# One explicit step order grouped by array tiling, and small matmuls padded to the whole array, in a fused attention and token-mixing kernel

## The chip, the cores and the metric

The kernel runs on one core of a Trainium2 chip. The metric is the device time of that core in microseconds (us), the median of several executions, lower is better. Ratios between kernels are computed as the mean time of one kernel's fast runs over the mean time of the other's fast runs in the same rounds on the same chip, so they are not quite the ratios of the medians quoted beside them. The square brackets after a ratio are its 95% interval. A single-core run is called slow when it lies over 1.5% above the fastest run of the same kernel.

The engines are called as the profile calls them: PE multiplies matrices, PEld loads its weights, DVE and ACT are the vector and scalar engines, POOL is the third elementwise engine, SP issues the DMAs (transfers between the chip's large memory and the engines' own). PSUM is the memory that PE writes its results to; copying a result out of it by ACT or DVE is called an eviction.

## The reference, cut to what matters

```python
# q, k, v: (8 batches, 8 heads, 576 positions, 64)
def _attn_ref(q, k, v):
    q_d, k_d, v_d = (means over 4 neighbouring positions)        # 144 positions
    out_d  = softmax(q_d k_d^T / 8) v_d                           # coarse attention
    out_up = np.repeat(out_d, 4, axis=2)
    out_local = softmax(q k^T / 8 where |i - j| < 4) v            # a narrow band
    return out_up + out_local

def _moe_ref(x, w_q, w_k, w_out):                                 # x: (8, 576, 512)
    wq, wk = x @ w_q, x @ w_k                                     # 512 -> 64
    mixed = (wq @ wk^T / 8) @ x
    return np.maximum(mixed, 0.0) @ w_out
```

The kernel works in half precision. It uses that `(wq wk^T) x = wq (wk^T x)`, so it forms the 64x512 matrix `M2 = wk^T x` first.

## The kernel before

For each batch there are three stages, and three batches are in work at a time: stage A of batch i runs together with stage B of batch i-1 and stage C of batch i-2. One such round is called a period here.

| stage | steps (name of the PSUM tile in the profile) |
|---|---|
| casts | POOL turns q, k and v from fp32 to fp16 |
| A | `tq`, `tk`, `tr`: transposes (pq, pk, pr); `sums`: coarse q and k by POOL; `score`: masks, then banded scores (psc); `vd`: coarse v (pv) |
| B | `cs`: coarse scores (pcs); `av`, `ca`: the two attention outputs (pav, pca); `odt`, `xt`: transposes (pod, px) |
| C | `wt` (pw), `wkt` (pwk), `wks` (pwd), `m2` (pm), `mx` and `mxr` (pmx, pmr), `og` and `ol` (po, pol) |

The PE can run as one array of 128x128 or as several smaller tiles. Which form a matmul uses follows from its shape: `wt` runs in 128x128, banded scores in 64x64, coarse scores in 64x128. The profile prints this form behind the operands of every matmul.

Four parts of the program carry the argument. First, only the PE is held to program order; the instructions of ACT, DVE and POOL are ordered by the build's own scheduler:

```python
class _InOrder:
    def __getattr__(self, name):
        f_ = getattr(self._engine, name)
        return lambda *a, **k: self._tc.keep_in_program_order(f_(*a, **k))
...
TEN_ = _InOrder(tc, nc.tensor)
```

Second, the PSUM buffers: every large step takes one of only three two-bank buffers, and the buffer comes free when ACT or DVE has copied it out.

```python
ps2 = ctx.enter_context(tc.tile_pool(name="ps2", bufs=3, space=bass.MemoryType.PSUM))   # ps(): two banks
ps1 = ctx.enter_context(tc.tile_pool(name="ps1", bufs=2, space=bass.MemoryType.PSUM))   # psm(): one bank
```

Third, the order of the steps. Each step has a weight, and `merge` interleaves the three stages so that each advances evenly through the period:

```python
return [(2., wt), (.5, wkt), (.4, wks), (1.5, m2), (.5, mx(0)), (.5, mx(1)), (.3, mxr),
        (1.8, og(0)), (1.8, og(1)), (.9, ol)]
...
for i in range(B + 2):
    ... m_ = [stage_c(i - 2), stage_b(i - 1), stage_a(i), stage_cast(i + 1)]     # shortened
    merge(m_)
```

Fourth, the two POOL steps and the matmul:

```python
def vv():      # stage_cast: cast of v
    nc.gpsimd.tensor_copy(v16[:, :, :, 0:64], v32)
def sums():    # stage A: coarse q and k; reads qT and kT, which tq, tk and tr produce
    nc.gpsimd.tensor_tensor(s_, t4[:, :, :, 0:2], t4[:, :, :, 2:4], op=ALU.add)
    ...
def vd():      # stage A: coarse v on the PE; reads the cast v
    pv = ps(name="pv")
    ...
```

The softmax here doesn't subtract the row's maximum and nothing guards it: scores larger than these inputs give would overflow.

## Time and profile before

The median of three runs was 227.92 us (227.62 to 228.11). In the middle of the run all periods are alike.

| reading, kernel before | value | view |
|---|---|---|
| span of the profiled run | 225.2 us | head of the page |
| period (start of `pw` to the next start of `pw`) | 23.06 us | chain of waits |
| PE, POOL, ACT, DVE busy in a period | 21.5, 13.6, 12.7, 12.1 us | table of windows |
| changes of array tiling in a period | 40 | PE's timeline, counted |
| gap before the first `pv` matmul, start to start | 0.79 us | PE's timeline |

The first lines are from the page of the kernel before: the busy time of each engine, with its share of the span and its instruction count, and the clock that PE was granted in 40 equal slices of the span (9 is 90% or more of full speed).

```profile
PE 180.7 (80%) x2752; PEld 112.2 (50%) x2752; DVE 104.3 (46%) x262; ACT 103.1 (46%) x137; POOL 115.9 (51%) x131
...
PEclk9999999857999999999999999999999999999999
```

The PE is by far the busiest engine, and its clock is full but for two slices early in the run. The next lines are the table of windows of the kernel before, for one period: the stretch and its length, busy time and count of each engine, then granted clock, DMA share and rate.

```profile
core 0: us, PE busy (x) PEld busy (x) DVE busy (x) ACT busy (x) POOL busy (x), PEclk, DMA share, GB/s
121.79:144.85 23.06, 21.51 (x344) 13.35 (x345) 12.07 (x28) 12.68 (x18) 13.57 (x13) 1.00 0.82 213
```

The PE is busy for 21.5 of 23.06 us at full clock. The chain of waits of the kernel before follows, for the same period: start in us, length, engine and what it worked on.

```profile
121.79 2.13 PE pw L27 x16
...
124.30 1.00 PE pq_2292 L27 x16
125.30 0.47 PE pca L27 x10
...
128.09 1.87 ACT kT L184
...
134.39 1.90 PE po L27 x8
136.29 0.99 PE pod L27 x8
137.28 0.69 PE psc L27 x36
138.21 1.83 PE po L27 x8
...
144.85 2.13 PE pw L27 x16
```

In this period PE holds 13.4 of the chain's 23.06 us, ACT and DVE hold 7.3. The long `po` steps of stage C stand between short steps of the other stages, and while the PE works at them the other engines have time to copy. Last, PE's timeline of the kernel before around `pv`: start, length, engine, operation, result<-operands, array tiling, shape, and in brackets the wait and what ended it.

```profile
117.37 0.23 PE L27 MATMUL px<-id_67,x_1811 128*128 128x128 f16 x1
117.44 0.22 PE L27 MATMUL px<-id_67,x_1898 128*128 128x128 f16 x1
...
117.88 0.22 PE L27 MATMUL px<-id_67,x_2135 128*128 128x128 f16 x1
118.67 0.38 PE L27 MATMUL pv<-v_1_138,P_149 128*32 128x512 f16 x1 [0.57 <-POOL v_1_138 L163]
```

Equal neighbours start about 56 ns apart (117.44 to 117.88 holds eight such steps), although each is shown as 220 ns long: matmuls overlap, so the distance from start to start is the cost. The last line: `pv` waits 0.57 us for POOL's cast of v, and so it does, by 0.5 to 0.6 us, in the other full periods.

### The profile page before, as it was taken

How to read it: one execution, taken by the hardware profiler on the slowest of the kernel's cores; microseconds unless marked ns; L12 is line 12 of the kernel's file. 1: busy time of each engine (PE TensorE's matmuls, PEld its weight loads, DVE VectorE, ACT ScalarE, POOL GpSimd, SP SyncE). 2: the span in 40 equal slices, each digit the busy share in tenths (PEclk: the TensorE clock that was granted, in tenths of full speed). 3: DMA queues.
4: the chain of work that ended last, by engine and by line, in shares of the span. 5: the costliest groups of instructions: out<-in, count | busy, mean ns of one | idle time of the engine just before them, and what ended most of it. 6: DMA issues, size and time to landing. Idle time of an engine off the chain costs nothing.

```text
span 225.2 us, 6421 instructions
## 1 busy us (share of the span) xinstructions
PE 180.7 (80%) x2752; PEld 112.2 (50%) x2752; DVE 104.3 (46%) x262; ACT 103.1 (46%) x137; POOL 115.9 (51%) x131
## 2 busy tenths in 40 slices
PE   0336077759988998899898989898989998999681
PEld 0223046536555664566455745574557455656330
DVE  6005046523466337354726472646364546477022
ACT  2154036413843593458444853475456554331331
POOL 3587991993079607970698059904990393000000
PEclk9999999857999999999999999999999999999999
DMA  6999989979974599659974997599731022104105
GB/s 184 288 198 328 317 165 263 266 150 243 249 173 146 156 349 163 194 146 341 170 207 129 332 175 167 189 309 206 195 136 27 3 92 82 41 3 157 53 0 210
DMA packets 74027, 40.54 MB, mean 180 GB/s; under 512 B 52432, under 2 KB 68880, under 8 KB 74000
## 3 DMA queue, kind: packets, MB, share of 16 engines
q1 hardware_dynamic: 73920, 40.12, 68.7%
q8 instruction: 21, 0.34, 0.7%
q14 instruction: 6, 0.05, 0.1%
q10 hardware_dynamic: 80, 0.03, 0.1%
HBM read 30.67 MB, written 9.44 MB: 178 GB/s over the span
## 4 chain that ended last, share of the span: by engine, by line
PE 49%; DVE 17%; POOL 16%; ACT 10%; issue 3%; DMA 3%; POOLq 0%; DVEq 0%; ACTq 0%
PE po L27 11%; PE pw L27 8%; ACT kT L184 5%; DVE xT L368 5%; DVE rmx L445 4%; PE pav L27 3%; PE pmx L27 3%; PE pod L27 3%; DMA q_72<-in_q_dram 3%; PE psc L27 3%; DVE os L470 3%; PE px L27 2%; PE pca L27 2%; POOL qd L207 2%; PE pwd L27 1%
## 5 line engine op out<-in xcount | busy, mean ns | idle before, releaser
L27 PE MATMUL po<-wo_98,rmx 128*128 128x512 f16 x128 | 30.4, 380 | 2.3 <-ACT rmx L443 0.6
L27 PEld LDWEIGHTS <-rmx 128*128 128x128 f16 (+1 forms) x160 | 14.1, 100 | 18.1 <-ACT rmx L443 0.7
L368 DVE COPY xT<-px 128x928 f16<-128x928 f16 (+1 forms) x32 | 14.3, 453 | 11.4 <-PE px L27 11.0
L348 DVE RECIPROCAL rz<-pav 128x8 f32<-128x8 f32 x40 | 8.1, 202 | 24.7 <-PE pav L27 23.9
L27 PEld LDWEIGHTS <-wqk_97 128*128 128x128 f16 x128 | 12.2, 100 | 6.5 <-DVE xT L368 2.9
L313 DVE RECIPROCAL rc<-pca 128x8 f32<-128x8 f32 (+1 forms) x16 | 3.2, 201 | 22.6 <-PE pca L27 22.6
L468 ACT COPY os<-po 128x1024 f32<-128x1024 f32 x8 | 8.1, 1012 | 11.8 <-PE po L27 10.6
L445 DVE TENSOR_SCALAR rmx<-pmx 128x1024 f16<-128x1024 f32 x8 | 9.8, 1224 | 7.3 <-PE pmx L27 7.3
L27 PE MATMUL pw<-odT,wqk_97 128*128 128x288 f16 x64 | 11.0, 297 | 1.5 <-DVE xT L368 1.5
L470 DVE COPY os<-po 128x1024 f32<-128x1024 f32 x8 | 9.7, 1216 | 4.8 <-ACT os L468 3.0
L443 ACT ACTIVATE rmx<-pmx 128x1024 f16<-128x1024 f32 x8 | 8.2, 1024 | 5.9 <-PE pmx L27 5.9
L27 PE MATMUL pw<-xT,wqk_97 128*128 128x288 f16 x64 | 10.8, 293 | 0.0
L27 PE MATMUL psc<-id_67,neg 64*128 64x232 f16 (+1 forms) x80 | 8.7, 280 | 2.1 <-DVE rmx L445 2.1
L329 DVE COPY odT<-pod 128x576 f16<-128x576 f16 x8 | 3.7, 458 | 14.4 <-PE pod L27 14.4
L27 PE MATMUL psc<-qT,kT 64*64 64x58 f16 (+1 forms) x640 | 10.3, 200 | 0.0
L482 ACT COPY ol<-pol 64x512 f32<-64x512 f32 x8 | 4.6, 579 | 11.6 <-PE pol L27 11.6
L27 PEld LDWEIGHTS <-kT 64*64 64x64 f16 x640 | 7.6, 114 | 4.4 <-issue 3.8
L27 PE MATMUL pq_230<-id_67,q_142 128*128 128x128 f16 x16 | 1.9, 312 | 8.6 <-POOL q_142 L156 8.6
L27 PE MATMUL pv<-v_0_136,P_149 128*32 128x512 f16 x3 | 1.3, 449 | 9.0 <-POOL v_0_136 L163 9.0
L27 PE MATMUL pol<-wo_98,rmx 128*64 128x512 f16 x32 | 8.4, 385 | 0.0
L242 ACT ACTIVATE E_0_122<-psc 128x928 f16<-128x928 f32 x4 | 3.8, 946 | 9.7 <-PE psc L27 9.7
L256 ACT CAST vd_0_195<-pv 128x512 f16<-128x512 f32 x4 | 2.4, 588 | 12.5 <-PE pv L27 12.5
(561 smaller groups left out, 518.3 us busy)
## 6 DMA issues: line engine op xcount, KB each, us to landing
out_dram<-os SPq DMA_DIRECT2D x16, 512.0 KB, 3.0
v_75<-in_v_dram SPq DMA_DIRECT2D x10, 128.0 KB, 4.2
v_215<-in_v_dram SPq DMA_DIRECT2D x10, 128.0 KB, 4.4
v_401<-in_v_dram SPq DMA_DIRECT2D x10, 128.0 KB, 3.7
v_779<-in_v_dram SPq DMA_DIRECT2D x10, 128.0 KB, 3.9
v_1258<-in_v_dram SPq DMA_DIRECT2D x10, 128.0 KB, 4.2
v_1737<-in_v_dram SPq DMA_DIRECT2D x10, 128.0 KB, 3.7
v_2216<-in_v_dram SPq DMA_DIRECT2D x10, 128.0 KB, 3.8
```

Of the source, the lines that this page charges most:

```text
L27: return lambda *a, **k: self._tc.keep_in_program_order(f_(*a, **k))
L184: nc.scalar.copy(t_[:, :, 0:512].rearrange("p j (t f) -> p j t f", f=4), g["p" + key].rearrange("p a (j f t) -> p (a j) t f", j=2, f=4))
L207: nc.gpsimd.tensor_tensor(qd, s_[:, :, :, 0], s_[:, :, :, 1], op=ALU.add)
L242: nc.scalar.activation(E.rearrange("p a n h w -> p a (n h) w")[:, :, :, 0:w], p_[:, :, 0:len(pr_) * W].rearrange("p a (x w) -> p a x w", w=w),
L329: nc.vector.tensor_copy(odT, p_[:, 0:4 * T].rearrange("p (r t) -> p r t", r=4))
L348: nc.vector.reciprocal(rz[:, n], _ap(p_, 64, [[row(p_), 128], [512, 2], [65, 4]]))
L368: nc.vector.tensor_copy(g["xT"][:, 2 * i:2 * i + 2, o:o + m * w].rearrange("p r (m w) -> p r m w", m=m), p_[:, :, lo:lo + 64 * m].rearrang ...
L443: nc.scalar.activation(d_, p_, ACTF.Relu)
L445: nc.vector.tensor_scalar_max(d_, p_, 0.0)
L468: nc.scalar.copy(os_, p_)
L470: nc.vector.tensor_copy(os_, p_)
L482: nc.scalar.copy(ol_, p_[0:64])
```

## The change

The intent: changing the form of the array costs PE time, and there are 40 changes in a period. The change writes all steps of all stages in one list, in which steps of equal tiling stand together, and it pads small matmuls so that they run in the form of their neighbours. The diff, cut to its core:

```diff
+    ORDER = [                                     # (offset of the batch, step)
+        (3, "load_qk"), (2, "load_v"), (0, "sums"),
+        (-2, "wt"),
+        (0, "mask0"), (-1, "cs0"), (0, "score0"), (-1, "av0"), (-1, "av3"),
+        (1, "tq"),
+        (0, "mask1"), (-1, "cs1"), (-2, "wks"), (-2, "wkt"), (0, "score1"), (-1, "av1"), (-1, "av2"),
+        (1, "tk"), (-1, "ca0"), (1, "tr"), (-2, "m2"),
+        (2, "cast_qk"),
+        (0, "mask2"), (0, "score2"), (-1, "av4"),
+        (-1, "ca1"), (-2, "mx0"), (-2, "mx1"), (-2, "mxr"), (-1, "xt0"), (-1, "odt"),
+        (1, "cast_v"),
+        (0, "vd"), (-1, "xt1"),
+        (-2, "og0"), (-2, "og1"), (-2, "ol"),
+    ]
...
-    for i in range(B + 2):
...
-        merge(m_)
+    for i in range(-1, B + 2):
+        for lag, name in ORDER:
+            b = i + lag
+            if 0 <= b < B and (b, name) not in done:
+                steps[b][name]()
```

The padding, one example of each kind (the coarse scores' tail, the summed keys, `mx`, `ol`):

```diff
-                        TEN_.matmul(p_[32 * hl:32 * hl + 32, p, 2 * T:3 * T],
-                                         kd[64 * p:64 * p + 64, hl, 128:160], ...          # 64x32
+                        pe.matmul(p_[:, p, 2 * T:3 * T],
+                                  kdt[64 * p:64 * p + 64, 128 * hl:128 * hl + 128], ...     # 64x128
-            for i, M in ((0, 128), (1, T - 128)):                                          # wks
-                    TEN_.matmul(p_[0:M, 64 * i:64 * i + 64],
+            for i in range(2):
+                    pe.matmul(p_[:, 64 * i:64 * i + 64],
-                    TEN_.matmul(p_[:, rr, :], M2[:, 128 * r:128 * r + 128], wT[0:64, 0:512], # mx
+                    pe.matmul(p_[:, rr, :], M2[:, 128 * r:128 * r + 128], wT[:, 0:512],
-                TEN_.matmul(p_[0:64], rmx[:, r, 512:S], wo16[:, r, :],                      # ol
+                pe.matmul(p_, rmx[:, r * S + 512:r * S + 640], wo16[:, r, :],
```

In the same way the second `ca` step and the `odt` transposes go from 16 rows to 128, and `m2` from 64 columns to 128. Loads of q and k are issued three batches ahead and of v two; before, all were one ahead.

## The prediction

> **What bounds the kernel now.** After the start, a batch takes 23.06 us: in the chain of waits `pw` starts at 98.73, 121.79, 144.85 us. The table of windows gives, for each such period, PE 21.5 us busy, POOL 13.6, ACT 12.7, DVE 12.1. PE in order is the bound. In PE's timeline, start to start, equal neighbours follow at about N/2.4 ns (512 columns 216 ns, 128 columns 56), but the last matmul before a change of array tiling holds PE some 95 ns longer (a transpose 151 instead of 56). The Trainium skill ("TensorEngine Tiling (Array Packing)", Key Properties) says that changing the tiling mode drains the engine; the trace agrees, with 95 ns. I count 40 changes a period: 3.8 us. Waits cost about 1.7 us more (`pv` on the cast of v 0.6, `psc` on `rmx` 0.3).
>
> **What the change removes and adds.** Explicit order and padding leave 11 changes a period: 29 fewer, -2.8 us. Padding costs little, since a matmul is paid by its moving columns: `odT` transposes +0.2 us (but eight changes gone), coarse scores +0.1. PE's own work would fall to about 19 us a period.
>
> **Why I do not expect that gain.** Only PE is held to program order. The built program shows how the other engines are ordered:
> - PSUM: three two-bank buffers. Before, long `po` and `pm` steps lie between short ones. Now the short ones that need ACT or DVE copies stand together: `wt`, cs0, score0, av0, av3, tq, cs1, score1, av1, av2, tk. ACT must do 0.64+0.89+0.95+1.87+0.64+0.26+0.8+0.95+1.87 = 8.9 us there, against about 6 us of PE work.
> - DVE: the copy `os` of the second output half (1.2 us) mostly stands in the next period, behind the `av` and `ca` evictions. It keeps one of the three buffers for some 20 us, so two rotate.
> - POOL: `sums` of batch i+1 (about 7.1 us, after `tr`) stands before the cast of v of batch i (2.3 us), for which `vd` of the same period waits.
>
> So a cycle closes: `vd` to `ol` 5 us, `wt` to `tr` about 13 us with the buffer waits (8.5 without), `rem` copy 0.6, `sums` 7.1, cast 2.3: up to 28.
>
> Estimate: both built orders with their waits, set end to end with durations from this trace. Kernel before: 22.6 a period (measured 23.06), so I add 2%. Kernel after: 25.8 to 28.6. The first `wt` comes at about 61 us instead of 51.8; five full periods, a short one (21), the last two stages 15 and 17 us: span about 255 us, plus 2.7 us that the time exceeds the span: **258 us**, 244 to 272. Faster by over 2%: 0.06, within 2%: 0.04, slower: 0.90.
>
> **What would show each step.** Right: changes of tiling in PE's timeline down to 11 a period; `pv` waits 2 to 4 us a period on POOL's cast of v; `pcs`, `pav`, `pca` wait on evictions by ACT and DVE, `os` copied by DVE some 15 to 20 us after its matmuls; PE busy below 80%; period 26 to 29 us. Wrong: periods of 19 to 21 us with PE over 90% busy.
>
> **What would make it wrong.** Slack in the buffers that I misread, or ACT and DVE copies overlapping more than before: then 23 us a period and a tie. Worse: PE idle for 4 us may lower its clock (PEclk was 0.5 to 0.8 in two early slices), which adds 1 to 2 us a period.

## The result, and the profile after

| | before, same rounds | after |
|---|---|---|
| median us | 227.83 | 273.51 (271.54 to 276.61, four runs) |
| ratio of fast runs | | 1.1975 [1.1909, 1.2042] |
| span of the profiled run | 225.2 | 272.1 |
| granted clock, mean | 0.975 | 0.884 |
| changes of tiling in a period | 40 | 11 |

The change made the kernel 20% slower. All outputs are right. The direction and the reasons of the prediction held, but the time lies 1.5 us outside the range, 15.5 us above the central figure. The table of the starts of `pw` shows where. These are differences of the start times in the two traces; the third row is what had been worked out for the prediction (its "25.8 to 28.6", with the 2% added that it names).

```
period between starts of pw    1      2      3      4      5      6      7
before                       23.84  23.06  23.06  23.06  23.06  23.06  16.30
after                        29.00  29.86  29.40  32.71  32.88  24.02  15.76
layout of the prediction     27.2   26.3   27.4   29.2   29.2   21.7   15.7
first pw: before 51.83 us, after 61.00 us, predicted 61
```

The single figures of the third row are not on record; its full periods span the 26.3 to 29.2 us that the prediction's text gives with the 2%. The start and the end came as predicted; 9.2 us of the loss arise before the first `pw`. Each of the first six periods is 1.8 to 3.7 us longer than laid out. The same two lines of the page as before, for the kernel after:

```profile
PE 183.6 (67%) x2752; PEld 122.0 (45%) x2752; DVE 109.4 (40%) x280; ACT 101.7 (37%) x129; POOL 115.3 (42%) x131
...
PEclk9999995599997989599599959899688886999998
```

The PE is busy for only 67%, and there are many slices with a clock digit of 5 to 8. The table of windows of the kernel after, first for two whole periods:

```profile
119.86:149.26 29.40, 22.49 (x345) 15.11 (x344) 12.17 (x29) 12.54 (x16) 13.11 (x12) 0.88 0.30 94
149.26:181.97 32.71, 23.38 (x345) 15.99 (x344) 12.17 (x29) 12.63 (x16) 13.97 (x13) 0.84 0.58 142
```

DVE, ACT and POOL have the same work as before, about 12, 12.6 and 13.5 us. PE's busy time is not lower but higher than the 21.5 us of before, although 29 changes of tiling are gone. The clock column says why: at full clock the same PE program was busy for 19.46 us, as a pinned version shows below. The same view of the kernel after, for parts of the second of these periods:

```profile
144.50:157.60 13.10, 10.37 (x147) 6.58 (x145) 3.42 (x10) 5.68 (x7) 5.17 (x6) 1.00 1.03 252
157.80:164.50 6.70, 5.32 (x113) 4.90 (x113) 1.80 (x4) 3.49 (x7) 0.00 (x0) 0.50 0.55 155
164.70:174.70 10.00, 5.36 (x81) 3.30 (x79) 7.08 (x17) 3.07 (x4) 9.01 (x9) 1.00 0.16 56
175.00:178.00 3.00, 2.92 (x18) 1.65 (x18) 1.05 (x3) 0.59 (x1) 3.00 (x3) 0.50 0.38 87
```

The clock is either 1.00 or 0.50 in these stretches. The chain of waits of the kernel after covers the same period:

```profile
144.55 0.56 PE px L27 x10
145.11 3.45 PE po L27 x16
...
155.32 1.07 PE pq_2428 L27 x16
156.47 1.88 ACT qT L182
158.38 0.44 PE pcs L27 x4
158.90 0.38 ACT Ec_2452 L296
...
161.95 1.82 PE pk_2555 L27 x16
163.77 0.87 PE pca L27 x10
165.46 2.10 POOL sum_2762 L203
...
172.76 2.27 POOL v_2_144 L166
175.08 1.16 PE pv L27 x4
176.24 1.07 PE px L27 x10
177.31 3.97 PE po L27 x16
...
182.13 1.98 PE pw L27 x16
```

Three things are to be seen. First, the chain leaves the PE for POOL from 165.46 to 175.08 us, through `sums` and the cast of v: for 9.6 us; the chain of the kernel before does not touch POOL in the period shown. Second, `pcs` (158.38) waits for ACT's copy of qT, because the PSUM buffer that it needs comes free with it. Third, equal work takes different times: 16 transposes are 1.07 us at full clock (`pq`) and 1.82 us at half (`pk`); `px` is 0.56 and 1.07; `po`, of which only the first part falls in the cold stretch, 3.45 and 3.97; `pca`, 0.47 in the kernel before and 0.87 here. These four alone lose 0.75 + 0.51 + 0.52 + 0.40 = 2.2 us in this period.

The longest waits of the PE in the steady part confirm the first two readings. This view of the kernel after shows what the PE waited for, with total us, times, and longest:

```profile
PE pv L27 <- POOL v_2_144 L166: 8.6, 2, 4.6
PE pv L27 <- POOL v_0_140 L166: 7.5, 2, 4.1
...
PE pcs L27 <- ACT qT L182: 5.1, 3, 1.7
```

Finally, the late copy of the second output half by DVE. The lines are from the timelines of the kernel after, PE's and then DVE's:

```profile
144.95 3.62 PE L27 MATMUL po<-wo_98,rmx_236 128*128 128x512 f16 x16
...
171.10 1.22 DVE L478 COPY os<-po 128x1024 f32<-128x1024 f32 x1
```

The matmuls end at 148.6 us and the copy starts at 171.1. For 22.5 us one of the three large PSUM buffers is blocked. In the kernel before, the same copy started at 142.06 us after matmuls that ended at about 140.0.

### The profile page after: what moved, and what is told of

Same layout as the page of the kernel before. It is cut to its first block, busy times and chain, and to the rows that moved or that the text cites. A ratio compares the mean times of both kernels' runs of the same rounds, so it can differ in the third digit from the quotient of the medians.

```text
span 272.1 us, 6476 instructions
## 1 busy us (share of the span) xinstructions
PE 183.6 (67%) x2752; PEld 122.0 (45%) x2752; DVE 109.4 (40%) x280; ACT 101.7 (37%) x129; POOL 115.3 (42%) x131
## 4 chain that ended last, share of the span: by engine, by line
PE 45%; POOL 22%; ACT 13%; DVE 6%; issue 5%; SPq 4%; DMA 2%; POOLq 1%; ACTq 0%; DVEq 0%
PE po L27 12%; PE pw L27 6%; ACT qT L182 3%; POOL qd L205 3%; PE pav L27 3%; PE pol L27 3%; SPq L101 3%; POOL v_0_140 L166 3%; PE pca L27 2%; PE pv L27 2%; PE px L27 2%; PE pcs L27 2%; POOL v_2_144 L166 2%; DMA v_79<-in_v_dram 2%; POOL v_1_142 L166 1%
## 5 line engine op out<-in xcount | busy, mean ns | idle before, releaser
L27 PE MATMUL po<-wo_98,rmx_251 128*128 128x512 f16 x64 | 16.4, 412 | 0.7 <-ACT rmx_251 L451 0.6
L27 PE MATMUL po<-wo_98,rmx_236 128*128 128x512 f16 x64 | 16.5, 418 | 0.0
L27 PEld LDWEIGHTS <-wqk_97 128*128 128x128 f16 x128 | 12.5, 98 | 5.3 <-issue 0.9
L27 PEld LDWEIGHTS <-rmx_251 128*128 128x128 f16 x80 | 8.1, 105 | 11.0 <-issue 2.3
L27 PEld LDWEIGHTS <-rmx_236 128*128 128x128 f16 x80 | 8.3, 105 | 10.0 <-issue 2.8
L27 PE MATMUL psc<-qT,kT 64*64 64x58 f16 (+1 forms) x640 | 11.5, 205 | 1.0 <-issue 1.0
L27 PE MATMUL pw<-odT,wqk_97 128*128 128x288 f16 x64 | 10.4, 286 | 0.0
L27 PEld LDWEIGHTS <-kT 64*64 64x64 f16 x640 | 8.7, 117 | 3.8 <-issue 2.3
L203 POOL TENSOR_TENSOR sum_2306<-qT 128x1152 f32<-128x1152 f16 x1 | 2.1, 2105 | 19.5 <-DVE qT L193 19.5
L203 POOL TENSOR_TENSOR sum_3212<-qT 128x1152 f32<-128x1152 f16 x1 | 2.1, 2106 | 18.8 <-DVE qT L193 18.8
L203 POOL TENSOR_TENSOR sum_2762<-qT 128x1152 f32<-128x1152 f16 x1 | 2.1, 2104 | 15.8 <-DVE qT L193 15.8
L203 POOL TENSOR_TENSOR sum_1839<-qT 128x1152 f32<-128x1152 f16 x1 | 2.1, 2106 | 15.2 <-DVE qT L193 15.2
L27 PEld LDWEIGHTS <-P_185 128*32 128x32 f16 x24 | 0.8, 95 | 16.8 <-issue 16.8
```

## The experiments

Two theories compete. **Waits**: the order of the steps ties the engines into a cycle (POOL's `sums` and cast of v; PSUM buffers that come free late), the PE idles, and idling lowers its clock on top. **PE work**: the padding or the new order costs the PE itself more than the changes of tiling save. They differ on what happens when padding and order are applied separately, and when only the order of the *other* engines is mended.

Pinning an engine means wrapping it as the PE is wrapped, so that its instructions keep program order. In all pinned kernels this is the edit, with the engine exchanged and the first iteration as given:

```diff
+class _Pin:
+    on = False
+    def __getattr__(self, name):
+        f_ = getattr(self._engine, name)
+        return lambda *a, **k: self._tc.keep_in_program_order(f_(*a, **k)) if _Pin.on else f_(*a, **k)
...
+    gpsimd_ = _Pin(tc, nc.gpsimd)                 # and vector_, scalar_ where named
-            nc.gpsimd.tensor_copy(v16[:, :, :, 0:64], v32)
+            gpsimd_.tensor_copy(v16[:, :, :, 0:64], v32)
...
     for i in range(-1, B + 2):
+        _Pin.on = i >= 1
```

The table gathers all runs. The ratio is to the kernel before in the same rounds; periods 2 to 5 are the full ones, worked out from the starts of `pw` in each trace.

| kernel | median us | ratio [95%] | periods 2 to 5, us | changes of tiling per period |
|---|---|---|---|---|
| before | 227.83 | 1 | 23.1, 23.1, 23.1, 23.1 | 40 |
| after | 273.51 | 1.1975 [1.1909, 1.2042] | 29.9, 29.4, 32.7, 32.9 | 11 |
| padding alone | 224.85 | 0.9876 [0.9826, 0.9927] | 22.8 each | 22 |
| order alone | 282.0 | 1.2382 [1.2305, 1.2458] | 30.7, 31.0, 33.8, 33.6 | 27 |
| after, POOL pinned | 251.37 | 1.0955 [1.0843, 1.1067] | 23.9, 28.7, 28.8, 29.6 | 11 |
| after, DVE pinned | 252.24 | 1.1064 [1.0987, 1.1142] | 30.2, 25.2, 24.4, 26.4 | 11 |
| after, both pinned | 232.33 | 1.0209 [1.0152, 1.0265] | 22.1, 25.2, 24.4, 26.4 | 11 |
| after, filler matmuls | 264.35 | 1.1654 [1.1597, 1.171] | 26.6, 30.6, 30.7, 30.7 | 11 |
| another order, all pinned | 216.64 | 0.9448 [0.9358, 0.9538] | 21.5, 24.2, 20.5, 19.5 | 14 |
| the same, nothing pinned | 236.81 | 1.0389 [1.0313, 1.0464] | 21.8, 27.7, 28.9, 28.0 | 14 |
| before, POOL pinned | 223.57 | 0.9836 [0.9797, 0.9875] | 22.4 each | 40 |
| before, POOL and DVE pinned | 223.93 | none given | 22.25 each | 40 |
| padding alone, both pinned | 217.1 | 0.9568 [0.9527, 0.9609] | 21.5 each | 22 |

### Padding without the order

The step functions of the kernel after, with the lists of weights, the loads and the start of the kernel before:

```diff
-    for i in range(-1, B + 2):
-        for lag, name in ORDER:
-            ...
+    for i in range(B + 2):
+        ...                                        # merge() of the kernel before, same weights
```

> The padded matmuls of the changed kernel, issued in the step order, start-up and load order of the kernel before. Changes of array tiling fall from 40 to 22 a period. Theory (padding is nearly free, a change of tiling costs about 95 ns, the loss comes from the new order): faster than before, 221 to 226 us; the 1.7 us a period that 18 changes are worth is partly eaten by waits, so about 0.6 to 1.5 us a period shorter than 23.06. Rival (padding makes PE's work dearer and is part of the loss): 228 us or more.

It ran in 224.85 us against 227.85, a ratio of 0.9876 [0.9826, 0.9927]. Padding does not cost time; it gains 1.2%. The 18 changes that it removes, at 94 ns each in this trace, are 1.7 us, but the period falls by only 0.22 us, from 23.06 to 22.84, less than the 0.6 to 1.5 us expected. PE's busy time fell by 1.33 us (21.51 to 20.18), and its idle time grew by 1.1 us. The largest part of that came at one place: the gap before the first `pv` matmul grew from 0.79 to 1.27 us. The rest is waits for copies, as of `pmx` on M2. So a shorter PE stream now runs into something that was already there before. That became a question of its own, taken up below.

### The order without padding

The list of steps of the kernel after, with the unpadded matmuls of the kernel before:

```diff
-                    pe.matmul(p_[:, rr, :], M2[:, 128 * r:128 * r + 128], wT[:, 0:512],
+                    pe.matmul(p_[:, rr, :], M2[:, 128 * r:128 * r + 128], wT[0:64, 0:512],
 ... (all padded matmuls likewise)
```

> The new step order with the unpadded matmuls of the kernel before: about 26 changes of tiling a period instead of 11. Theory (the order alone makes the loss): as slow as the changed kernel or a little slower, 272 to 280 us. Rival (padding makes the loss): back to 225 to 235 us.

It ran in 282.0 us, a ratio of 1.2382, slower than with padding, and 2 us beyond the range expected. Together with the run above this settles it: the loss comes from the order (with its start-up and its earlier loads, which came with it), and the padding works against it. The theory that padded work is the cost has fallen.

### POOL pinned

In the program of the kernel after, the cast of v of a batch stands before `sums` of that batch. The build put it behind even the `sums` of the next batch. Pinning POOL (from iteration 1) is the whole edit.

> The changed kernel with POOL alone held to program order from the second iteration on, so that the cast of v no longer stands behind the sums of the next batch. Theory (three causes: POOL order, the late os copy on DVE, too few free PSUM buffers): the wait of pv on POOL's cast of v goes to zero, and the time falls by a half of the loss or less, to 248 to 258 us. Rival (PSUM buffers alone set the period, POOL's wait only hides in it): within 3 us of 273.5.

The time fell by 22 us, to 251.37 (two of the four runs, the profiled one too, were slow: 251.43 us at a clock of 0.915). POOL's timeline of this kernel shows the cast of v ahead of `sums`, and what POOL waited for:

```profile
146.67 2.32 POOL L40 CAST v<-v 128x2560 f16<-128x2560 f32 x1 [5.71 <-PE pav L27]
150.10 2.10 POOL L40 TENSOR_TENSOR sum<-qT 128x1152 f32<-128x1152 f16 x1 [1.11 <-DVE qT L208]
```

The cycle over POOL is open. Among the longest waits of the PE in this trace there is none of `pv` on the cast. Periods 3 to 5 still take 28.7 to 29.6 us, so it is not the only cause. The copy `os` by DVE is as late as in the kernel after, by 21 to 23 us in three batches, so this run changes POOL's order alone.

### DVE pinned

> The changed kernel with DVE alone held to program order from the second iteration on, so that the copy of the second output half stands right behind its matmuls and frees its PSUM buffer. Theory: periods fall from about 29 to 33 us to about 24 to 27, time 245 to 258 us; pcs and pav wait less on evictions. Rival (POOL's order alone makes the loss): within 3 us of 273.5.

The time fell by 21 us, to 252.24. The next lines are one of the chain of waits and one of DVE's timeline of this kernel:

```profile
167.24 3.55 PE po L27 x16
...
170.83 1.22 DVE L40 COPY os<-po 128x1024 f32<-128x1024 f32 x1 [1.67 <-PE po L27]
```

The copy now starts as soon as the matmuls are done, where it lagged 22.5 us before. The wait of `pv` remains in periods 1 and 2: 9.5 us in all, in two waits of up to 5.3 us. These two periods gained nothing (29.8 and 30.2 us, against 29.0 and 29.9). From period 3 on `pv` waits no more: POOL's timeline shows two casts of v in one period, at 111.96 and 118.45 us, and from then on the cast ends 15 to 21 us before `pv`. POOL was not pinned here; the build changed its order together with DVE's. So this run does not isolate the late copy.

### POOL and DVE pinned

> The changed kernel with POOL and DVE both held to program order from the second iteration on. Theory: both engine orders together made most of the loss; what is left is the crowd of short steps in front of ACT, with three PSUM buffers: periods of about 23.1 to 24.5 us in my layout from trace durations, time 230 to 240 us, so a tie or slightly slower than before, in spite of 29 changes of tiling fewer. If the crowd of short steps costs nothing: 205 to 212 us.

The time fell to 232.33 us, by 41 us. That is nearly the sum of the two single gains (22 and 21), but the sum proves nothing, since pinning DVE had mended POOL's order as well: periods 3 to 5 are the same in both runs (25.2, 24.4, 26.4 us). DVE's order is isolated by the comparison with POOL pinned in both: from 251.37 to 232.33 us it is worth 19 us, or 17 by the ratios. What remains is a ratio of 1.0209. The largest waits of the PE that are left, after the start, are all on ACT: `pk` waits 3.6 us in four times on the exponentials, `pav` 3.2 us in six on those of the coarse scores, `px` 3.1 us in seven on `rmx`. These are the copies of the short steps that now stand together. One full period of this run was at full clock throughout, and its line in the table of windows gives PE's own work in the new order:

```profile
80.84:102.97 22.13, 19.46 (x345) 13.20 (x344) 12.27 (x30) 12.48 (x16) 19.11 (x20) 1.00 0.96 239
```

The PE program is that of the kernel after. So PE's own work did fall, from 21.5 to 19.46 us, and what the PE was busy above that in the kernel after, 1.3 to 4.6 us in each of its periods 1 to 5, came with the half clock.

### Filler matmuls before `pv`

What does the clock cost by itself? The PE can be kept busy while it waits for the cast of v, with matmuls whose result is overwritten:

```diff
     pv = ps(name="pv")
+    for _ in range(14):
+        pe.matmul(pv[:, 1, :], id16, wo16[:, 0, :], start=True, stop=True)
```

> The changed kernel with 14 extra, unneeded matmuls of 512 columns (3.0 us at full clock) into the buffer of pv, overwritten after, in the time in which PE waits for the cast of v. Theory (the half-clock windows after that wait cost 1 to 2 us a period over and above the wait itself): 5 to 12 us faster than the changed kernel, 261 to 268 us, and a granted clock of 0.92 or more against 0.884. Rival (the lower clock costs nothing, since PE waits anyway): the same or slower, 273 to 282 us.

It ran in 264.35 us. That is 9.2 us less than the kernel after by the medians, or 7.3 us by the two ratios ((1.1975 - 1.1654) x 227.4 us; the two were timed in different rounds), although it adds about 3 us of work to each of the eight batches. The lines are from the timelines of this kernel, POOL's and then PE's; the last is the clock line of its page:

```profile
144.17 2.33 POOL L166 CAST v<-v 128x2560 f16<-128x2560 f32 x1
...
169.37 3.19 PE L27 MATMUL pv<-wo,id 128*128 128x512 f16 x14
172.49 0.41 PE L27 MATMUL pv<-v,P 128*32 128x512 f16 x4
...
PEclk9999999579999997999689995999779999999999
```

The true `pv` matmuls follow at full clock, the stretches at half clock shrink from 65.2 us in the trace of the kernel after to 36.9 us (summed over the records of the granted clock), and the mean clock rose from 0.884 to 0.934. But the filler did not do what it was meant for. The cast of v that these `pv` matmuls read had ended at 146.5 us, 26 us before them: from the fourth batch on the build placed the cast 19 to 26 us ahead of `pv`, so there was no wait left to fill. The copy `os` also came earlier, 7 to 12 us behind its matmuls in three batches instead of 21 to 23. POOL's order, DVE's order and the clock all changed at once, so the gain of 7 to 9 us is not the price of the clock, nor a bound for it. That price is read from the trace of the kernel after instead, in the section on the prediction.

### Another order of the same steps, all engines pinned

If the order is the fault and not the idea of grouping, another order should keep the gain. This one has 14 changes of tiling a period. It puts long steps (`og1`, `og0`, `wt`) between the short ones, places the cast of v in the program well over a period before the `vd` that needs it, and pins POOL, DVE and ACT from iteration 3:

```diff
     ORDER = [
-        (3, "load_qk"), (2, "load_v"), (0, "sums"),
-        ...
+        (3, "load_qk"), (2, "load_v"), (-1, "av1"), (1, "cast_v"), (-1, "av2"), (-2, "wt"), (0, "mask2"),
+        (0, "sums"), (0, "score2"), (0, "mask0"), (-1, "av3"), (0, "score0"), (-1, "av4"), (-2, "wkt"),
+        (-2, "wks"), (-1, "cs0"), (-1, "cs1"), (2, "cast_qk"), (-1, "av0"), (-2, "m2"), (-1, "ca0"),
+        (0, "mask1"), (0, "score1"), (-1, "ca1"), (-2, "mxr"), (-2, "mx0"), (-1, "xt1"), (-2, "mx1"),
+        (-1, "odt"), (1, "tq"), (0, "vd"), (-2, "og1"), (1, "tk"), (-2, "og0"), (-1, "xt0"),
+        (-2, "ol"), (1, "tr"),
     ]
```

> The padded matmuls, POOL, DVE and ACT in program order from iteration 3 on, and another order of the steps: long matmul steps (wt, m2, og0, og1, ol) stand between the short ones so that evictions keep up; about 14 changes of tiling a period, not 11. Theory (grouping is worth its 95 ns a change only if the evictions are spread): periods of 19.5 to 20.5 us, time 205 to 215 us, faster than both kernels. Rival (the three-buffer PSUM rotation or the DMA issue sets a floor of about 23 us whatever the order): 228 us or more.

It ran in 216.64 us, a ratio of 0.9448 [0.9358, 0.9538], and beats both kernels, though the median is 1.6 us beyond the range expected. Its best period is 19.48 us. (Two of four runs, the profiled one too, were slow; the interval uses the fast two.) The period of 24.19 us has another cause. The lines are from POOL's timeline and from the table of windows of this kernel:

```profile
94.84 2.32 POOL L40 CAST v<-v 128x2560 f16<-128x2560 f32 x1 [13.34 <-DMA v<-in_v_dram]
...
90.00:130.00 40.00, 36.13 (x619) 23.38 (x621) 20.20 (x49) 22.28 (x30) 27.16 (x24) 0.96 0.95 253
```

The cast waited 13.3 us for the load of v, and the DMA engines are busy for 95% of that stretch. The chain of waits of this period runs through SP's issues and the landing of this load, then through the cast and `sums`. So the loads are the limit there; whether it is their issue or their transfer is not shown.

### The same order, nothing pinned

> The same order of steps as spread_a, but POOL, DVE and ACT left to the scheduler as in the changed kernel. Theory (the scheduler's order of the other engines by itself costs 4 to 5 us a period in later iterations): 226 to 242 us. Rival (a good order of steps is enough): within 3 us of spread_a.

With the identical PE order, but with the other engines left to the build, it takes 236.81 us, a ratio of 1.0389. The order of the other three engines alone is worth 20 us here, or 21 by the ratios, which come from the same rounds. (The profiled run was slow, 238.43 us.) This is the clearest result: PE's order and the other engines' order have to be chosen together.

### The kernel before, POOL pinned

The wait of 0.57 us in the kernel before, and the small gain of the padding, suggested that the kernel before was itself partly held by the same cycle.

```diff
+    gpsimd_ = _Pin(tc, nc.gpsimd)
-            nc.gpsimd.tensor_copy(v16[:, :, :, 0:64], v32)
+            gpsimd_.tensor_copy(v16[:, :, :, 0:64], v32)
 ... (all POOL instructions of the casts and of sums likewise)
     for i in range(B + 2):
+        _Pin.on = i >= 2
```

> The kernel before, unchanged but for POOL held to program order from iteration 2 on, so that the cast of v stands one period earlier. Theory (the kernel before was itself held by the cycle tr, sums, cast of v, pv, so PE alone did not set its period): the 0.79 us gap in front of pv goes to 0.1, periods fall from 23.06 to about 22.3 us, time 221 to 225 us. Rival (PE alone sets the period): within 1 us of 227.5.

It ran in 223.57 us, a ratio of 0.9836 [0.9797, 0.9875]; the period fell from 23.06 to 22.4 us with the PE's instructions unchanged. PE's busy time stayed (21.51 and 21.49 us), its idle time fell by 0.6 us, and the wait of `pv`, 0.57 us, is gone. So PE in order was not the whole bound of the kernel before: most of these 0.65 us of each period was the cycle from `tr` over `sums` and the cast of v to `pv`. (The build also put DVE's copy `os` 2 us earlier, behind its matmuls at once; its share is not separated.)

### The kernel before with POOL and DVE pinned, and padding with both pinned

These two tell what the padding is worth once that cycle is open. The edit is `_Pin` on POOL and DVE from iteration 2, in the kernel before and in the padding-only kernel.

> The kernel before with POOL and DVE held to program order from iteration 2 on. About as before_pin_pool, at most 1.5 us faster: 220 to 225 us. It is the partner of pad_pin_pd, for the price of the changes of tiling.

> pad_only (padded matmuls in the step order of the kernel before: 22 changes of tiling a period instead of 40) with POOL and DVE held to program order from iteration 2 on. Theory (in pad_only the 1.7 us of removed drains were mostly turned into waits, of which the one for the cast of v was the largest): periods of about 21.0 to 21.5 us, 0.8 us or more shorter than before_pin_pd, time 211 to 217 us. Rival (changes of tiling hardly matter even when PE does not wait on POOL): 0.3 us a period or less, time 220 us or more.

The first ran in 223.93 us; two of its runs were slow, so no ratio is given, and its fast runs are 222.19 and 221.64 us. The second ran in 217.1 us (216.67 to 218.67, all four fast), a ratio of 0.9568 [0.9527, 0.9609] to the kernel before. The head of the page of the second gives the engines' busy time, PE's busy share in the 40 slices, and its clock:

```profile
PE 170.2 (79%) x2752; PEld 110.9 (52%) x2752; DVE 108.3 (50%) x280; ACT 102.8 (48%) x129; POOL 116.3 (54%) x131
...
PE   0336049639989998999899989998999899999681
...
PEclk9999999985999999999999999999999999999998
```

The PE is busy for 80 to 90% and more of every slice of the steady part, at full clock. With both pinned the period is 22.25 us without padding and 21.52 with it. So padding is worth 0.73 us a period where it was worth 0.22. Even so that is less than half of the 1.7 us that its 18 removed changes cost: PE's busy time falls by 1.3 us (21.49 to 20.19), so some 0.4 us must be paid for the padding itself (an estimate, the difference), and its waits grow by 0.57 us to 1.33, short ones on copies (of `pmx` on M2 and of `pw` on xT 0.35 us each, of `psc` on rmx 0.38 us).

## Why the prediction was right or wrong

**The price of a change of tiling: right.** The prediction said 95 ns. From start to start, at full clock and without waits, the excess at a change over the pace of equal neighbours (N / 2.4 + 2.5 ns for N columns) has a median of 96 ns in the trace of before, 94 ns with padding alone and 95 ns in the trace of after. The Trainium skill ("TensorEngine Tiling (Array Packing)", Key Properties) says only that a change of mode drains the engine. The count fell from 40 to 11 a period, as predicted.

**The gain that would not come: right.** The three named reasons were each found. The order on POOL: `pv` waited 3.5 us a period on the average (17.3 us in five waits), and pinning POOL alone gave back 22 us. The late copy by DVE: 22.5 us late, somewhat more than the 15 to 20 said; with POOL pinned, pinning DVE too gave back 17 to 19 us. The crowded evictions: `pcs` waits for ACT's copy of qT up to 1.7 us, and the order that spreads the evictions, with its engines pinned, reached a period of 19.5 us. In the same rounds it has a ratio of 0.9448 against 1.0209 for the kernel after with POOL and DVE pinned, 17 us; as ACT was pinned too in the one and not in the other, how much of that is the crowding is not separated. The Trainium skill ("TensorEngine Tiling (Array Packing)", PSUM Bottleneck) warns that "Tiling speeds up TensorE but not PSUM evacuation". The trace shows the like for steps that are not tiled: 16 transposes in 128x128 take the PE 1.07 us, their copy to qT takes ACT 1.88 us.

**The start and the end: right.** The first `pw` came at 61.00 us, as said, and the last short period took 15.76 us for 15.7.

**The term that was mis-sized: the clock.** The prediction set the periods at 25.8 to 28.6 us (26.3 to 29.2 with its 2%) and mentioned under "what would make it wrong" that "PE idle for 4 us may lower its clock", "which adds 1 to 2 us a period". It stood outside the sum, and it was sized too small. Measured full periods were 29.0 to 32.9 us, 1.8 to 3.7 us more than laid out for the same period. The trace of the kernel after accounts for that. Where its chain of waits runs through PE in a stretch at half clock, half of that time is the clock's doing, since equal work took twice as long there (107 ns from transpose to transpose against 56). Worked out so from the chain and the records of the granted clock, an estimate:

| period | 1 | 2 | 3 | 4 | 5 | 6 |
|---|---|---|---|---|---|---|
| lost to the half clock on the chain, us | 1.4 | 3.9 | 1.9 | 3.4 | 3.6 | 2.5 |
| longer than laid out, us | 1.8 | 3.6 | 2.0 | 3.5 | 3.7 | 2.3 |

That is 16.8 us against 16.9. With it the prediction of 258 us would read about 275, against 273.51 measured. So the waits, in sum, were laid out rightly, and the missing term is the clock: 1.4 to 3.9 us a period where "1 to 2" stood, and stood outside the sum. No experiment isolates it, since the filler run failed to; the trace shows it, period by period.

The mistake of method is plain: waits of 2 to 4 us a period had been predicted, and a falling clock after waits of that size is what the Trainium skill tells ("TensorE: Matmul & The Clock Gate", Part 1: half rate after an idle window of about 3.4 us). If the waits were in the sum, their price on the clock belonged in the sum too.

**What bounds the kernel before: incomplete.** "PE in order is the bound" missed about 0.6 us of each period that POOL's order held, as the pinned version of the kernel before shows. The 0.57 us wait of `pv` stood in the prediction's own list, as a small loss, not as a sign of the cycle that the change would then stretch.

**PE's own work of about 19 us: right.** At full clock the PE was busy for 19.46 us in a period of the same PE program, with 11 changes. In the kernel after itself the half clock hid this.

## What to carry to other kernels

Removing a cost from the busiest engine pays only as far as no cycle through the other engines is nearly as long; a short wait that repeats in every period, like the 0.57 us here, shows where the next bound is. When one engine is held to program order, look at the order that the build gives to the others, and pin them too if it works against you: with the same PE order that was worth 20 us here (236.81 to 216.64). Steps of equal form should be grouped only as far as the buffers allow: put long matmul steps between those that wait for a copy, and count waits of several microseconds at more than their length, since the half clock can follow them. And after every edit look at the built order of the engines that were not touched: pinning DVE alone, and adding the filler, each changed POOL's order too, and only the traces told.

Two versions beat both kernels by over 4%: the padding with POOL and DVE pinned (217.1 us) and the other order with all pinned (216.64 us, but with a wider spread). Their intervals overlap, so neither is called better.

## What the Trainium skill lacked or had wrong

- "TensorEngine Tiling (Array Packing)", Key Properties, gives no figure for the drain at a change of tiling mode. It measured 94 to 96 ns from start to start beyond the pace of equal neighbours (medians of three traces), against 56 ns for a 128-column matmul between equal neighbours.
- "TensorE: Matmul & The Clock Gate", "Why this matters for your kernels", advises against PE-idle gaps over about 3 us. That single-gap rule is not enough: the half clock from 157.8 to 164.5 us in the trace after came with no single gap over 2 us around it, only several short ones (1.96 us from start to start at `pcs` the longest). The same page's section on PSUM-queue cycling does tell of a clock that oscillates through short idle times, but with no length or share that would let one estimate it; here it was 65.2 us at half clock in a span of 272.1 us. The trace of the kernel after tells the share. Its clock changes only at marks 3.41 us apart; take PE as active while columns stream, by the measured pace of N / 2.4 ns at full clock and N / 1.2 ns at half. Of the stretches between two marks at full clock, the 11 that a half clock followed were active for 43% or less (39% from 154.3 to 157.7 us), the 40 that full clock followed for 42% or more. Of those at half clock, the 10 that full clock followed were active for 78% or more, the 8 others for 66% or less. Over all 13 traces both borders hold within a few per cent, at 39 to 46% and 68 to 71%.
- The same page, Part 2, "Back-to-back issue gap", gives a sustained rate for streams in which every matmul has its own weight load: about 81 ns for 128 columns and about 131 ns for 512. The traces here do not agree. Every matmul has its weight load (2752 of each), and at full clock 16 matmuls of `po` with 512 columns took 3.45 us, 216 ns each, and ten transposes of `px` 0.56 us, 56 ns each: the page's formula for the isolated gap, N / 2.4 + 2.5 ns, is what held.
- The same page, Part 4, says that the full rate does not engage for transposes. Transposes (written with `pe.transpose`) ran at 56 ns from start to start here, the full rate. Whether they count as activity that keeps the clock up was not tested by itself.
- No page read says that pinning one engine to program order leaves the others to the build, nor what that can cost: 20 us of 237 in the pair with identical PE order.
